# An S4 convolution block with its backward pass: one PSUM pool, fewer table operations, state sums split between VectorE and TensorE

## The chip, the cores and the metric

The kernel runs on one core of one Trainium2 chip. A core has five engines that work side by side and wait for each other through semaphores: TensorE (PE: matmuls, with its weight loads shown as PEld), VectorE (DVE), ScalarE (ACT), GpSimd (POOL) and SyncE (SP). Each takes its own instructions strictly in order. Sixteen DMA engines move data between HBM and the on-chip memory SBUF; here SP's queue issues most transfers and POOL's queue most stores of results. Matmul results land in PSUM, eight banks of 2 KB a partition (512 fp32 numbers), from which only DVE and ACT can read ("eviction"). The metric is the device time of one execution in microseconds (us), the median of the runs.

## The reference

The reference computes a block and all its gradients. `L` = 2048 rows, `D` = 512 channels, `N` = 128 states, `F` = 1792.

```
xn  = layernorm(x)
K[d,l] = Re sum_n C[d,n] * exp(dt[d]*A[d,n]*l) * dt[d]*B[d,n]     # complex A, B, C
s   = irfft(rfft(xn, 4096) * rfft(K, 4096))[:2048] + xn * Dskip   # per channel
g   = silu( silu(xn @ w1) @ w2 )
out = x + s * g
grads of x, A_re, A_im, B_re, B_im, C_re, C_im, log_dt, Dskip, w1, w2 for a given grad_out
```

Inputs and outputs are bf16.

## The kernel before, in words

**Stages.** The channels are taken in four blocks `b` of 128. First come the layer norm (`layer_norm`) and constants (`make_consts`: the transform's sines `TF`, their transposed form `TI`, selection matrices). Then, per block, `gen_tables` makes powers of `exp(dt*A)`: a phase is multiplied out into the scratch area `AR` as int32, shifted so that only the fraction of a turn is left, turned into sine and cosine by one ACT instruction, and multiplied by magnitudes that were stored in HBM. From a few powers (`E`, `Y`, `H`) products give all that the kernel `K` needs; matmuls `ps_k` and `ps_e` sum over the states. `gen_conv_x` transforms a block of `xn` and stores the spectrum in HBM (`Ud`); `gen_conv_fwd` transforms `K`, loads the spectrum (`sp_in`), multiplies (`products`, lines 1046 on) and transforms back. The transforms (`dft_fwd`, `dft_inv`) are two matmul steps each with evictions between (`ps_s`, `ps_i`), and a turn of the middle result by DMA or by PE. Beside all this `gen_ffn_fwd` runs the two forward matrix products (`ps_h`, `ps_o`), 256 rows at a time.

In the middle the gates are formed (`gen_gate_rows`), and the backward convolution (`gen_conv_bwd`, which loads both spectra again) runs beside the backward products `ps_da` and `ps_dx` (`gen_ffn_da`).

Last comes the gradient of the states (`gen_ssm_bwd`): per block `ssm_fold` sums the gradient of `K` into 21 exponents by matmuls with 0/1 matrices and evicts them four times repeated (`Gf`); `ssm_half` multiplies by two masks (`Gb`); then in 16 groups `ssm_v` multiplies by transposed powers (`ps_v`, evicted to `Vb`), `ssm_products` forms four products with `E` (`Tp`, a real and an imaginary pair for every exponent), and `ssm_sums` adds them up over the exponents by 43 matmuls with the identity into `psS`. `gen_ssm_grads` ends each block. Beside it run the weight gradients `gen_dw2` and `gen_dw1` (both `ps_w`; the second reads `dh_tok`, loaded by DMA transposes), and, after the states, the gradient of the layer norm (`gen_ln_bwd`).

**Pools.** PSUM has two pools: `pf`, four tiles of one bank, and `pc`, two tiles of two banks. SBUF pools open and close on a left and a right side; a pool that opens where another one closed waits for it. `gen_ln_bwd` uses a pool on the right, where the states' pool `sb` is. The transforms share four `w8` tiles, used in turn.

**Order.** The body (lines 1743 to 1887) only records operations. `Plan` then simulates the engines with fixed costs and sets the order on every engine, which engine takes an operation recorded as "any" (a copy on DVE or ACT), and which PSUM bank a tile gets. It starts from a random order, improves it by backward and forward passes (`FROM`, `ROUNDS`, `FIRST`, `LAST`), and applies a list of 175 random shifts of priorities, `NUDGES`. The resulting order is fixed in the program. All instructions are issued through one line of `Recorder.emit`, so nearly every row of the profile names L158 (line 158); rows are told apart by the names of their tiles.

Of the kernel before, what the change touches and what calls it, by code (L numbers as in the profile page):

```python
# [12 lines left out]
ACT = mybir.ActivationFunctionType  # L13
# [3 lines left out]
I32 = mybir.dt.int32  # L17
DRAM = bass.MemoryType.DRAM
PSUM = bass.MemoryType.PSUM
P = 128  # L20
PI_LO = 3.1415925
PB = 18
# [70 lines left out]
class Recorder:  # L93
# [13 lines left out]

    def noted(self, engine, op):
        def note(*args, **kw):
            self.ops.append((engine, op, args, kw))  # L110
        return note

    def emit(self, tc, roots, order=None, homes=None, engines=None, heads=None):
# [40 lines left out]
        for n in order or range(len(self.ops)):  # L154
            engine, op, args, kw = self.ops[n]
            if engine == "any":
# [5 lines left out]
        for line in sorted(marks.values(), key=lambda l: l[0][0].space is not None):  # L162
            while line:
                step(line)
# [3 lines left out]
class Plan:  # L168
# [5 lines left out]
    FROM, ROUNDS = (2182906552, 1, 0), 4  # L174
    FIRST, LAST = (22000.0, 3000.0, 1500.0, 80.0, 1200.0), (20660.199999999997, 3000.0, 1500.0, 80.0, 1200.0)
    NUDGES = [(1090443319, 3, 4000), (4118025466, 5, 1000), (1691718919, 5, 2000), (1436320375, 0, 200), (2213169401, 5, 2000),
# [1763 lines left out]
```

## Time and profile before

| | us |
|---|---|
| median of 3 runs | 594.05 |
| lowest, highest run | 593.77, 594.74 |
| span of the profiled execution | 592.6 |
| PE busy in it | 543.2 |
| DVE busy | 519.2 |
| ACT busy | 434.1 |
| POOL busy | 75.8 |

The span runs from the first to the last instruction of the profiled execution. A row of the groups by shape reads: line, engine, operation, output <- inputs, shapes, xcount | busy us of all, mean ns of one | idle us of the engine before them and what ended it. The mean is one instruction's latency; busy divided by the count is smaller, since neighbours overlap. A row of the windows reads: the window, its length, then busy us and (x instructions) of PE, PEld, DVE, ACT and POOL, then the granted PE clock, the DMA engines' busy share, and GB/s. A row of the chain reads: start us, us, engine, tile, line, xcount. A row of waits reads: who waited <- for whom: us in total, times, longest us.

### The profile page before, as it was taken

How to read it: one execution, taken by the hardware profiler on the slowest of the kernel's cores; microseconds unless marked ns; L12 is line 12 of the kernel's file. 1: busy time of each engine (PE TensorE's matmuls, PEld its weight loads, DVE VectorE, ACT ScalarE, POOL GpSimd, SP SyncE). 2: the span in 40 equal slices, each digit the busy share in tenths (PEclk: the TensorE clock that was granted, in tenths of full speed). 3: DMA queues.
4: the chain of work that ended last, by engine and by line, in shares of the span. 5: the costliest groups of instructions: out<-in, count | busy, mean ns of one | idle time of the engine just before them, and what ended most of it. 6: DMA issues, size and time to landing. Idle time of an engine off the chain costs nothing.

```text
span 592.6 us, 14999 instructions
## 1 busy us (share of the span) xinstructions
PE 543.2 (92%) x6208; PEld 400.4 (68%) x6208; DVE 519.2 (88%) x955; ACT 434.1 (73%) x541; POOL 75.8 (13%) x161
## 2 busy tenths in 40 slices
PE   0579999999999995799999999999999999999997
PEld 0456657758567764677667667677887777795586
DVE  9999999999999989999998898468998956387794
ACT  6989899988998989997888858165467454673652
POOL 8131010101001000000001000000002033101221
PEclk9989999999999997799999999999999999999999
DMA  9978999999999989678789965989999999397795
GB/s 225 366 242 247 262 223 361 259 272 319 272 329 268 356 273 318 193 249 189 235 249 308 249 206 163 237 233 167 218 218 270 196 208 272 102 200 204 230 230 145
DMA packets 187029, 144.64 MB, mean 244 GB/s; under 512 B 120080, under 2 KB 167952, under 8 KB 183376
## 3 DMA queue, kind: packets, MB, share of 16 engines
q1 hardware_dynamic: 180528, 125.59, 80.6%
q0 software_dynamic: 6144, 17.83, 9.3%
q8 instruction: 48, 0.79, 0.5%
q10 hardware_dynamic: 288, 0.26, 0.1%
q14 instruction: 21, 0.17, 0.1%
HBM read 55.97 MB, written 58.85 MB: 194 GB/s over the span
## 4 chain that ended last, share of the span: by engine, by line
PE 42%; DVE 11%; issue 2%; DMA 2%; ACT 2%; DVEq 0%; ACTq 0%; SPq 0%
PE ps_w L158 14%; PE ps_da L158 6%; PE ps_dx L158 6%; PE psS L158 5%; PE ps_i L158 4%; PE ps_v L158 3%; DVE sp_in L158 2%; PE pt_t L158 2%; DVE cm L158 2%; DVE g_t L158 1%; DMA sp_in<-Ud 1%; PE ps_s L158 1%; DVE dhT L158 1%; DVE Tp L158 1%; PE G L158 1%
## 5 line engine op out<-in xcount | busy, mean ns | idle before, releaser
L158 PEld LDWEIGHTS <-W 128*128 128x128 bf16 x1008 | 90.5, 99 | 23.9 <-issue 8.3
L158 ACT CAST dA<-ps_s 128x1024 bf16<-128x1024 f32 x85 | 85.3, 1036 | 8.8 <-PE ps_s L158 8.1
L158 PEld LDWEIGHTS <-xn 128*128 128x128 bf16 x512 | 47.9, 99 | 28.3 <-DVE xn L158 21.0
L158 PE MATMUL ps_o<-W,aT 128*128 128x512 bf16 x224 | 59.3, 384 | 3.4 <-ACT XT L158 3.2
L158 PE MATMUL ps_da<-doT,W 128*128 128x256 bf16 x448 | 61.6, 273 | 0.2 <-DVE dhT L158 0.2
L158 PE MATMUL ps_h<-XT,W 128*128 128x256 bf16 x448 | 59.2, 278 | 2.1 <-ACT hT L158 1.5
L158 PE MATMUL ps_dx<-W,dhT 128*128 128x512 bf16 x224 | 58.0, 379 | 0.0
L158 PE MATMUL ps_w<-YD,a_tok 128*128 128x512 bf16 x224 | 56.0, 379 | 0.2 <-ACT a_tok L158 0.2
L158 ACT CAST Vb<-ps_v 128x672 bf16<-128x672 f32 x55 | 38.0, 724 | 23.4 <-PE ps_v L158 14.9
L158 PE MATMUL ps_w<-dh_tok,xn 128*128 128x256 bf16 x448 | 54.1, 273 | 0.1
L158 DVE TENSOR_TENSOR Tp<-Vb,Eb 128x1344 bf16<-128x1344 bf16 x64 | 52.0, 857 | 2.1 <-ACT Vb L158 1.4
L158 PE MATMUL psS<-Tp,ident 128*128 128x128 bf16 (+1 forms) x688 | 47.4, 218 | 0.0
L158 ACT CAST dB<-ps_i 128x1024 bf16<-128x1024 f32 x39 | 38.4, 1017 | 12.1 <-PE ps_i L158 11.7
L158 DVE TENSOR_TENSOR dhT<-ps_da,dhT 128x512 bf16<-128x512 f32 x56 | 38.1, 688 | 8.1 <-PE ps_da L158 8.1
L158 PEld LDWEIGHTS <-ident 128*128 128x128 bf16 x688 | 41.7, 98 | 3.0
L158 PEld LDWEIGHTS <-TF 128*128 128x128 bf16 x384 | 27.6, 103 | 19.1 <-issue 11.3
L158 ACT CAST o<-ps_w 128x256 bf16<-128x256 f32 (+1 forms) x36 | 15.7, 440 | 31.7 <-PE ps_w L158 26.8
L158 PE MATMUL ps_i<-I,sp_in 64*128 64x128 bf16 x768 | 35.9, 220 | 1.4 <-DVE sp_in L158 1.2
L158 PEld LDWEIGHTS <-YD 128*128 128x128 bf16 x576 | 28.9, 98 | 7.9 <-issue 4.4
L158 PEld LDWEIGHTS <-sp_in 64*128 64x128 bf16 x768 | 28.0, 96 | 9.2 <-DVE sp_in L158 4.1
L158 PEld LDWEIGHTS <-aT 128*128 128x128 bf16 x224 | 19.8, 99 | 21.3 <-issue 5.6
L158 PE MATMUL ps_s<-dB,F 128*64 128x512 bf16 x192 | 30.5, 389 | 3.2 <-ACT dA L158 1.9
(225 smaller groups left out, 1197.0 us busy)
## 6 DMA issues: line engine op xcount, KB each, us to landing
Yd<-YD SPq DMA_DIRECT2D x8, 1024.0 KB, 6.4
sp_in<-Ud SPq DMA_DIRECT2D x8, 1024.0 KB, 6.2
Ed<-E SPq DMA_DIRECT2D x8, 672.0 KB, 4.1
Eb<-Ed SPq DMA_DIRECT2D x8, 672.0 KB, 5.6
h_in<-Hd SPq DMA_DIRECT2D x10, 512.0 KB, 4.3
Hd<-hT POOLq DMA_DIRECT2D x8, 512.0 KB, 7.2
Ud<-dA SPq DMA_DIRECT2D x4, 1024.0 KB, 7.1
KXd<-dA SPq DMA_DIRECT2D x4, 1024.0 KB, 6.7
```

The source lines that it names most:

```text
L158: getattr(getattr(nc, engine), op)(*[on(a) for a in args], **{w: on(a) for w, a in kw.items()})
```

## The change

- PSUM becomes one pool `pf` of eight one-bank tiles. Every two-bank tile of the transforms, of `ps_v` and of the fold is replaced by two one-bank tiles, each with its own eviction.
- `gen_conv_fwd` begins with `gen_conv_x` of its block and keeps the spectrum as `k.U`; it is still stored for the backward pass, and no longer loaded in the forward pass.
- Phases are scaled so that a turn is 2^16. The shift is dropped; ACT's sine reads the low 16 bits of each int32 directly. The same is done for the transform's sines. The quarter-turn offset may run on DVE or ACT, and so may the last step of the layer norm.
- `TI` is made by 32 PE transposes with four evictions in place of one DMA transpose.
- In `gen_tables` two pairs of product operations become two double-width ones, and the two halves of `W` one operation.
- `ssm_fold` evicts each exponent sum four times under a 0/1 scale straight into the masked form `Gb`, and its zeroing matmuls go; `ssm_half` makes only the second mask's half.
- `ssm_sums` first combines the real and imaginary products on DVE, in place, and then needs 21 matmuls; a later subtraction goes.
- `gen_ln_bwd`'s pool moves to the left side, beside the states; it writes its result in place, `pd_l` has two buffers instead of four, and `dh_tok` two instead of three.
- The planner gets other starting values, no longer counts an ordering that lies wholly within a tile's own users, and has a list of 28 `NUDGES`.

The core of the diff:

```diff
+    def any_affine(self, out, in_, scale, bias, held):
-    FROM, ROUNDS = (2182906552, 1, 0), 4
-    FIRST, LAST = (22000.0, 3000.0, 1500.0, 80.0, 1200.0), (20660.199999999997, 3000.0, 1500.0, 80.0, 1200.0)
+    FROM, ROUNDS = (3240493571, 0, 60), 5
+    FIRST, LAST = (30000.0, 5000.0, 3000.0, 120.0, 1200.0), (30000.0, 5000.0, 3000.0, 120.0, 1200.0)
...
-            gates = {g for n in u for g in self.shuts[n]}
+            gates = {g for n in u for g in self.shuts[n] if not set(self.order[g][0]) <= set(u)}
...
-        TS(out=ks[:, :, 1, :], in_=prod[:], scalar=8191, op=ALU.bitwise_and)
-        TS(out=prod[:], in_=prod[:], scalar=6144, op=ALU.add)
-        TS(out=ks[:, :, 0, :], in_=prod[:], scalar=8191, op=ALU.bitwise_and)
+        TS(out=prod[:, :, 0], in_=prod[:, :, 1], scalar=-16384, op=ALU.add)
...
-    nc.sync.dma_start_transpose(k.TI[:], k.TF[:].rearrange("p t c k -> p (t c k)"))
+    turned(k, lambda i: k.TF[:].rearrange("p t c k -> p (t c) k")[:, i], 32, k.TI, k.ev)
...
-        for h in range(2):
-            ps = pc.tile([P, 8, P], F32, name="ps_s1", tag="pc")
-            for j in range(8):
+        for h in range(4):
+            ps = k.pf.tile([P, 4, P], F32, name="ps_s1", tag="pf")
+            for j in range(4):
...
-            TS(out=V[:, 0, 0:n], in_=V[:, 1, 0:n], scalar=-float(1 << (PB - 2)), op=ALU.add)
-            TS(out=V[:, :, 0:n], in_=V[:, :, 0:n], scalar=32 - PB, op=ALU.logical_shift_left)
+            nc.any_affine(V[:, 0, 0:n], V[:, 1, 0:n], 1.0, -float(1 << (PB - 2)), k.quarter[:])
...
-            TT(out=m1, in0=lo(x[0]), in1=hi(x[1]), op=ALU.mult)
-            TT(out=m2[:], in0=lo(y[0]), in1=hi(y[1]), op=ALU.mult)
-            TT(out=out(c), in0=m1, in1=m2[:], op=op)
+            TT(out=area.rearrange("p (x m a) -> p x m a", m=8, a=4), in0=lo, in1=hi, op=ALU.mult)
...
+            TT(out=Y[:, c, :, 8:32, :].rearrange("p q j a -> p q (j a)"), in0=pr[0][:, :, c], in1=pr[1][:, :, 1 - c], op=op)
...
 def gen_conv_fwd(k, b):
+    yield from gen_conv_x(k, b)
...
-    U = spectrum_in(k, dft, b, "U")
+    U = k.U
...
-        k.ev(out=Gf[:, :, 16 * bank:16 * bank + n, :],
-                       in_=G21[:, bank, 0:32 * n].rearrange("p (e q) -> p q e", e=n).unsqueeze(3).to_broadcast([P, 32, n, 4]))
+        for h in range(2):
...
+            for a in range(4):
+                nc.any_affine(dst[:, :, :, a], src, k.m4[:, a:a + 1], 0.0, 0.0)
...
 def ssm_sums(k, Tp, out):
-    psS = k.pf.tile([P, 3, 64], F32, name="psS", tag="pf")
+    psS = k.pf.tile([P, 2, 64], F32, name="psS", tag="pf")
+    nc.vector.tensor_tensor(out=Tp[:, 0, :, 0], in0=Tp[:, 0, :, 0], in1=Tp[:, 1, :, 1], op=ALU.subtract)
+    nc.vector.tensor_tensor(out=Tp[:, 0, :, 1], in0=Tp[:, 0, :, 1], in1=Tp[:, 1, :, 0], op=ALU.add)
     for e in range(NE):
-        nc.tensor.matmul(out=psS[:, 0:2], lhsT=k.ident[:], rhs=flat(Tp[:, 0, e]), start=(e == 0), stop=False)
-    for r in range(2):
-        nc.tensor.matmul(out=psS[:, 1 + r:2 + r], lhsT=k.ident[:], rhs=flat(Tp[:, 1, 0, r:r + 1]), start=False, stop=False)
-    for e in range(1, NE):
-        nc.tensor.matmul(out=psS[:, 1:3], lhsT=k.ident[:], rhs=flat(Tp[:, 1, e]), start=False, stop=(e == NE - 1))
+        nc.tensor.matmul(out=psS[:], lhsT=k.ident[:], rhs=flat(Tp[:, 0, e]), start=(e == 0), stop=(e == NE - 1))
...
-        dh = fw.tile([P, k.T, 2, P], BF16, name="dh_tok", tag="dh_tok", bufs=3)
+        dh = fw.tile([P, k.T, 2, P], BF16, name="dh_tok", tag="dh_tok", bufs=2)
...
-    k.pf = ctx.enter_context(Room(nc, "pf", bufs=4, space=PSUM))
-    k.pc = ctx.enter_context(Room(nc, "pc", bufs=2, space=PSUM))
+    k.pf = ctx.enter_context(Room(nc, "pf", bufs=8, space=PSUM))
...
-        yield from woven([gen_tables(k, 0), gen_conv_x(k, 0)], [2, 1])
+        yield from gen_tables(k, 0)
         for b in range(1, 4):
-            yield from woven([gen_tables(k, b), gen_conv_x(k, b), gen_conv_fwd(k, b - 1)], [3, 1, 1])
+            yield from woven([gen_tables(k, b), gen_conv_fwd(k, b - 1)], [3, 1])
...
-    interleave([gen_ln_bwd(k, pool("lw", side="right")), dw], [1, 1])
+    interleave([gen_ln_bwd(k, pool("lw")), dw], [1, 1])
```

More of the change, by code (lines that the diff above doesn't have):

```diff
@@ L21 @@
 PI_LO = 3.1415925
-PB = 18
+PB = 16
 BR, SR, APART = 1.8, 0.5, 5
@@ L980, in dft_fwd @@
             continue
-        pt = pc.tile([P, 16, P], BF16, name="pt_f", tag="pc")
-        for j in range(16):
-            nc.tensor.transpose(out=pt[:, j], in_=A[:, u, j, :], identity=k.ident[:])
-        k.ev(B[:, u], pt[:])
+        for v in range(2):
+            pt = k.pf.tile([P, 8, P], BF16, name="pt_f", tag="pf")
+            for j in range(8):
+                nc.tensor.transpose(out=pt[:, j], in_=A[:, u, 8 * v + j, :], identity=k.ident[:])
+            k.ev(B[:, u, 8 * v:8 * v + 8], pt[:])
     for _ in range(LAG - 1):
@@ L1004, in dft_inv @@
     for q in range(4):
-        ps = pc.tile([P, 2, 4, 32, 4], F32, name="ps_i2", tag="pc")
+        ps = [k.pf.tile([P, 4, 32, 4], F32, name="ps_i2", tag="pf") for _ in range(2)]
         for g in range(4):
@@ L1396, in ssm_fold @@
         nc.sync.dma_start(GE[a:P:4].rearrange("p i t q -> p i (t q)"), k.dKd[b, a].rearrange("i j r -> j i r"))
-    G21 = pc.tile([P, 2, 512], F32, name="G21", tag="pc")
+    G21 = [k.pf.tile([P, 512], F32, name="G21", tag="pf") for _ in range(2)]
     ID, SH, WR, MX = 0, 1, 2, 3
```

150 lines of the change are left out of this document (79 added, 71 removed), and 40 rows, old and new, of the table NUDGES.

## The prediction

> **What bounds the kernel now.** I read the three stages first (windows), then what TensorE (PE) waits for, then the chain that ended last, then the groups of instructions by shape.
>
> ```profile
> core 0: us, PE busy (x) PEld busy (x) DVE busy (x) ACT busy (x) POOL busy (x), PEclk, DMA share, GB/s
> 0.00:240.00 240.00, 202.18 (x2379) 146.05 (x2380) 232.21 (x404) 213.70 (x272) 37.96 (x93) 0.97 0.95 286
> 240.00:390.00 150.00, 143.49 (x1769) 101.16 (x1767) 127.39 (x182) 108.23 (x112) 6.45 (x12) 0.99 0.82 231
> 390.00:593.00 203.00, 197.56 (x2065) 153.24 (x2063) 159.58 (x370) 112.21 (x159) 31.34 (x56) 1.00 0.92 204
> ...
> 205.00:262.00 57.00, 44.44 (x669) 35.12 (x666) 52.00 (x76) 51.58 (x55) 1.12 (x2) 0.88 0.75 247
> ```
>
> There are three regimes. To 240 us (tables, forward convolution, forward feed-forward) VectorE (DVE) is busy 232.2 of 240 us, 97%, and ScalarE (ACT) 89%: both are full, and PE loses 38 us. From 240 to 390 PE is at 96%. From 390 to the end PE is at 97% while DVE has 43 us and ACT 91 us to spare. The hole at 205 to 262, where the last forward convolution hands over to the backward pass, has PE idle for 12.6 us with DVE and ACT at 91%.
>
> ```profile
> PE pt_t L158 <- DVE xn L158: 20.7, 2, 20.1
> ...
> 532.72 2.36 PE psS L158 x43
> ...
> 557.86 24.26 PE ps_w L158 x205
> 582.19 7.16 PE ps_w L158 x64
> ```
>
> PE's only long named wait is the first one, 20.1 us for the layer norm. The chain's end is pure matmul: the state sum of one group is 43 matmuls in 2.36 us, 54.9 ns each, and 31 us of weight gradient close the run. So in the last stage work taken from PE is time, and in the first stage only work taken from DVE and ACT together is.
>
> **Complex sums ahead of TensorE.** Of the 43 identity matmuls of a group 21 stay: 22 x 16 groups x 54.9 ns = 19.3 us of PE go. The fold loses its zeroing matmuls, 4 x (512 + 160) columns at the same 0.43 ns a column, 1.15 us, and gains four small ones: 1.0 us. Together -20.3 us. In exchange DVE gets two in-place operations of 1344 elements per group.
>
> ```profile
> L158 DVE TENSOR_TENSOR Tp<-Vb,Eb 128x1344 bf16<-128x1344 bf16 x64 | 52.0, 857 | 2.1 <-ACT Vb L158 1.4 <-issue 0.5
> L158 DVE TENSOR_TENSOR Gb<-Gf,MK 128x2688 bf16<-128x2688 bf16 x8 | 12.4, 1556 | 0.0
> L158 DVE TENSOR_TENSOR Sa<-Sa 128x256 f32<-128x256 f32 x4 | 1.7, 425 | 8.7 <-ACT Sa L158 8.7
> L158 DVE TENSOR_TENSOR AR<-tau,ecst 128x1024 int32<-128x1024 f32 x8 | 9.8, 1219 | 0.0
> ```
>
> The nearest row is Tp, the same size and type: 52.0 / 64 = 0.81 us, so 32 x 0.81 = 26.0 us. The upper bound is the rate of the slow AR row (1.19 ns an element): 1.60 us, 51 us in all. I take 26.0. DVE gives back half of Gb (8 x (1.55 - 0.81) = 5.9) and the Sa subtraction (1.7). DVE in the last stage: 159.6 + 26.0 - 7.6 = 178.0 us, while PE's end would shrink that stage to 203 - 20.3 = 182.7. That is 97%, beside a PE that is as full, and hardly an order keeps both so busy. But copies that may go to either engine sit there too.
>
> ```profile
> L158 DVE CAST Vb<-ps_v 128x672 bf16<-128x672 f32 x9 | 7.6, 856 | 4.5 <-PE ps_v L158 4.5
> L158 DVE CAST o<-ps_w 128x512 bf16<-128x512 f32 x3 | 2.1, 689 | 11.1 <-PE ps_w L158 11.1
> L158 DVE CAST Gf<-G 128x640 bf16<-128x640 f32 x2 | 1.6, 815 | 0.0
> ```
>
> These 11.3 us on ACT bring DVE to 166.7, 91%. The sums also put 1.6 us of DVE between a group's products and its psS matmuls: a new wait on PE. PE takes its matmuls in order, so behind a late psS stand the next ps_v, for whose eviction ACT and then DVE's next products wait, and ps_w. With two streams (weight gradients and states) to order around that I charge 4 us; bounds 0 and 13 (the 178 us at the 91% that DVE keeps in the hole is 195.6, against 182.7).
>
> **Sines of low halves, fewer table operations.** The shift of the phases goes altogether, the twiddle masks shrink from three operations to one per half, and the pairs of products and of W are merged.
>
> ```profile
> L158 DVE TENSOR_SCALAR AR<-AR 128x2048 int32<-128x2048 int32 x8 | 9.8, 1226 | 0.0
> L158 DVE TENSOR_SCALAR AR<-AR 128x1920 int32<-128x1920 int32 x8 | 9.3, 1160 | 0.0
> L158 DVE TENSOR_SCALAR ks<-prod 128x1024 int32<-128x1024 int32 x4 | 2.7, 684 | 0.0
> L158 DVE TENSOR_SCALAR prod<-prod 128x1024 int32<-128x1024 int32 x2 | 1.4, 690 | 0.0
> L158 DVE TENSOR_TENSOR AR<-YD,H 128x1536 bf16<-128x1536 bf16 x16 | 15.2, 958 | 0.0
> L158 DVE TENSOR_TENSOR m<-YD,H 128x1536 bf16<-128x1536 bf16 x16 | 15.2, 959 | 0.0
> L158 DVE TENSOR_TENSOR W<-E,CT 128x1344 bf16<-128x1344 bf16 x32 | 27.0, 861 | 0.0
> L158 DVE TENSOR_SCALAR xn<-x_sb,rstd,nb 128x512 bf16<-128x512 bf16 x16 | 5.7, 399 | 0.0
> ```
>
> Shift: 9.8 + 9.3 = 19.1 us off DVE. Twiddles: 2.7. Products: Tp to Gb gives 0.52 ns an element, so 3072 cost 1.71 us busy; 16 of them, 27.4, replace 30.4: 3.0. W: 16 at Gb's 1.55 us, 24.8: 2.2. Sum 27.0 us off DVE before 240. The layer norm's rows (xn) and the phase offset may now go to ACT; a 512-wide row costs 0.36 us here against 0.77 for the scaled ACT row below, and I leave them on DVE, at no change; moved, they would take up to 12.3 us of ACT for 5.7 of DVE. The sines read as many elements as before, from a 16-bit half at every second place; no row shows that, and I take no change.
>
> **PSUM as one pool of eight banks.** Every two-bank tile becomes two one-bank tiles with an eviction each.
>
> ```profile
> L158 ACT CAST dA<-ps_s 128x1024 bf16<-128x1024 f32 x85 | 85.3, 1036 | 8.8 <-PE ps_s L158 8.1 <-ACT dK L158 0.4
> L158 ACT CAST hT<-ps_h 128x512 bf16<-128x512 f32 x48 | 27.0, 608 | 3.7 <-PE ps_h L158 2.0 <-DMA Hd<-hT 1.7
> L158 ACT CAST Vb<-ps_v 128x672 bf16<-128x672 f32 x55 | 38.0, 724 | 23.4 <-PE ps_v L158 14.9 <-DVE Tp L158 4.0 <-issue 2.4
> L158 ACT CAST Xr<-ps_k 128x336 bf16<-128x336 f32 x22 | 10.1, 460 | 1.9 <-PE ps_k L158 1.9
> L158 ACT CAST Gf<-G 128x2048 bf16<-128x2048 f32 x4 | 7.5, 1866 | 7.2 <-PE G L158 7.1
> L158 ACT ACTIVATE AR<-AR,m,rstd 128x512 bf16<-128x512 bf16 x16 | 12.3, 812 | 2.5 <-DVE m L158 2.5
> ```
>
> One 1024-column eviction is 85.3 / 85 = 1.00 us; two of 512 are 2 x 0.56 = 1.12. In the first stage 92 tiles are split (64 of the forward transforms, 24 of the inverse, 4 transposes): 11.0 us more on DVE and ACT. [...] In the last stage 64 splits of Vb cost at most 2 x 0.46 - 0.69 = 0.23 us each, 15 us, and 64 masked evictions of 256 or 80 elements replace Gf (9.1 us in the rows shown): each below the 0.77 us of the 512-wide scaled row, so 49 us at most, 29 by the Xr row's 0.46. With 91 us to spare on ACT I take both as hidden; without that slack they would cost 35 us. The middle stage's 76 splits, 9.1 us, hide in the 22.6 us of DVE and 41.8 of ACT that are idle there. What eight interchangeable banks save is not in the trace: at most the 6.5 and 5.4 us that PE idles in the middle and last stages, at least nothing. I take nothing.
>
> First stage in sum: DVE and ACT together 445.9 - 27.0 + 11.0 + 4 (four 1024-wide evictions for the TI table) = 433.9. At the present joint share the 240 us become 233.5: -6.5. Bounds: -22 (DVE alone binds: 232.2 - 27.0 + 5.5 = 210.7, at 97% 217 us) and +11 (ACT alone binds and takes the 15: 228.7 at 91%).
>
> **Input spectrum on chip.** Four reloads go, and the transform of the input moves into the convolution that uses it.
>
> ```profile
> sp_in<-Ud SPq DMA_DIRECT2D x8, 1024.0 KB, 6.2
> TI<-TF SPq DMA_TRANSPOSE x1, 12.0
> ...
> 197.89 0.32 SPq L158 DMA_DIRECT2D Ud<-dA  x1
> 213.53 2.35 DVE L158 TENSOR_TENSOR cm<-sp_in,dA 128x2048 bf16<-128x2048 bf16 x2
> ```
>
> The loads, four of 6.2 us, and the TI transpose of 12.0 leave SP's queue; none of them is a wait of PE in the view of waits, so nothing is gained, and TI's 32 transposes on PE (1.8 us at psS's pace) fall into its first idle 20 us. What is late next is the spectrum: it now holds one of four `w8` slots until the inverse transform has read the product made in it. Block 3's spectrum was stored at 197.9 us, ahead of block 2's products at 213.5; now its first tile must wait for those to be consumed, and behind its matmuls on PE stand those of the feed-forward. Its 16 evictions move into the hole at 205 to 262, where DVE and ACT are at 91%: 16 x 0.56 / 2 = 4.5 us there, won back earlier. I charge 2; bounds 0 and 10.
>
> **Norm gradient beside the state sums.** Its pool moves to the left so that its DVE work need not wait for the states' end; without that the 91% above could not be spread. The price is `dh_tok` at two buffers instead of three.
>
> ```profile
> 557.45 8.42 SPq L158 DMA_TRANSPOSE dh_tok<-DHd  x2
> 568.17 8.78 SPq L158 DMA_TRANSPOSE dh_tok<-DHd  x2
> ...
> dh_tok<-DHd SPq DMA_TRANSPOSE x14, 6.9
> ```
>
> A step of the gradient takes 64 matmuls, 7.16 us. Its two transposes take 8.42 us to issue and 6.9 to land, 15.3 us; behind them on SP's queue stand the last loads and stores. With two buffers a bare step stalls up to 15.3 - 7.16 = 8.1 us. Seven steps spread among 150 us of other PE work hide this; only the last can be bare. I charge 2; bounds 0 and 8.
>
> **Sum.** -20.3 + 4 - 6.5 + 2 + 2 = -18.8; the middle stage I leave as it is. The profiled span 592.6 becomes 573.8; the median of the runs stands 1.45 above that span, so 575.
>
> **Rivals.** *The first stage follows DVE alone.* For it: 97% against ACT's 89%, and 0.95 of the DMA engines' time, eased by four loads. Against: the copies are already dealt between both engines. -22 in place of -6.5 gives 560; with free banks worth 4 more, 556. *DVE takes over the tail.* If the copies stay on DVE: 178.0 us at 91% is 195.6, +13 in place of +4, and without the first stage's gain 591; half of that gain leaves 587. *The transposes bind (slower).* If the state work is finished early and the weight gradient is left alone at the end, each bare step costs 8.1 us; 18.8 + 2 lost is the point where it decides, three bare steps. Three give 575 - 2 + 24.3 = 597, four 605. For it: 31 us of pure weight gradient end the run now, and DMA is at 0.92. Against: those steps now run with no stall. *No change.* The order comes from a new search of the planner. PE's 38 us lost before 240 and 12.6 in the hole are what an order decides; one that loses 19 more gives 594.
>
> **How the numbers follow.** Forecast 0.52 (575, its own range 566 to 583), DVE-only first stage 0.19 (556), DVE tail 0.15 (587), transposes 0.10 (about 600), no change 0.04. The shown runs differ by 0.16%, so 0.2% is about what can be told from none. Faster 0.86, same 0.04, slower 0.10. The range 557 to 590 leaves out about half of the 556 case, the slower one and no change.
>
> **What would show it.** psS at 336 matmuls; two new Tp rows near 0.81 us; in the last stage DVE above 88% and PE still above 95%. No int32 shift rows, ps_s at 512 columns near 0.56 us. DVE before 240 clearly under 97%. Waits of PE on `dh_tok` or of the ps_s transform on a released `sp_in` slot would be the costs I charged; a new DVE row at 1.6 us, or PE under 90% in the last stage, would make the forecast wrong.

## The result and the profile after

The changed kernel takes **619.36 us** (618.16 to 619.45, four runs) against 594.15 us (593.77 to 594.74) for the kernel before on the same chip: 1.0415 of its time, 95% interval 1.040 to 1.043. It is 4% slower. The forecast was 575 us, range 557 to 590: wrong in size and in sign. In the changed kernel nearly all rows name L169, in the kernels of the experiments L160 or L172; it is the same line of `Recorder.emit`. Profiled spans are 1.5 to 1.9 us shorter than the times.

I cut the span at two places that both kernels have: the first `ps_da` (the backward products begin) and the first `G` (the fold of the state gradient begins). In the kernel before, the cut at 260.0 lies 0.2 us ahead of its first `ps_da`. Windows by these stages, of the kernel before:

```profile
0.00:260.00 260.00, 217.97 (x2632) 158.92 (x2633) 251.67 (x432) 232.13 (x289) 38.52 (x94) 0.97 0.92 278
260.00:388.50 128.50, 126.20 (x1502) 87.04 (x1500) 107.94 (x154) 89.70 (x95) 5.90 (x11) 1.00 0.85 238
388.50:592.60 204.10, 199.06 (x2080) 154.49 (x2078) 159.58 (x370) 112.30 (x159) 31.34 (x56) 1.00 0.92 205
```

And of the changed kernel:

```profile
0.00:265.60 265.60, 233.40 (x2700) 177.70 (x2700) 240.87 (x407) 237.33 (x370) 36.83 (x93) 0.96 0.87 260
265.60:403.30 137.70, 137.62 (x1485) 99.73 (x1483) 113.59 (x172) 91.88 (x145) 6.49 (x12) 1.00 0.75 209
403.30:617.60 214.30, 186.43 (x1701) 138.96 (x1701) 175.72 (x407) 126.98 (x268) 31.42 (x56) 0.94 0.88 193
```

Every stage is longer: by 5.6, 9.2 and 10.2 us. In the first two PE is busy 26.9 us more, though the change added no matmul there but the 32 transposes of `TI`, and the order moved about 20 others ahead of the first `G`. In the last it is busy 12.6 us less and the stage is longer all the same. These rows of the groups say that most instructions came at the prices of the prediction:

```profile
L169 ACT CAST dA<-ps_s 128x512 bf16<-128x512 f32 x162 | 86.7, 640 | 3.5 <-PE ps_s L169 3.4
L169 DVE TENSOR_TENSOR AR<-YD,H 128x3072 bf16<-128x3072 bf16 x16 | 27.7, 1752 | 0.0
L169 DVE TENSOR_TENSOR W<-E,CT 128x2688 bf16<-128x2688 bf16 x16 | 24.8, 1552 | 0.8 <-DMA Kd<-KE 0.8
L169 DVE TENSOR_TENSOR Tp<-Tp 128x1344 bf16<-128x1344 bf16 x32 | 26.6, 848 | 0.0
L169 PE MATMUL psS<-Tp,ident 128*128 128x128 bf16 x336 | 25.3, 223 | 6.5 <-DVE Tp L169 6.5
L169 ACT ACTIVATE Gb<-G,m 128x80 bf16<-128x80 f32 (+1 forms) x57 | 27.1, 688 | 7.5 <-DVE Gb L169 6.4 <-PE G L169 1.0
```

The 32 sums cost 26.6 us (26.0 forecast), an eviction of 512 columns 86.7 / 162 = 0.535 us (0.56), the double-width products 27.7 us (27.4), `W` 24.8 (24.8), and `psS` has its 336 matmuls. One group the prediction took as hidden: the masked evictions `Gb`, 27.1 us on ACT alone. What changed for TensorE shows only in single matmuls. The first step of the inverse transform (`ps_i<-I`, 1024 matmuls of 64 rows in all), a stretch of it in the timeline, before:

```profile
128.79 0.22 PE L158 MATMUL ps_i<-I,cm 64*128 64x128 bf16 x2
128.85 0.22 PE L158 MATMUL ps_i<-I,sp_in 64*128 64x128 bf16 x2
128.91 0.22 PE L158 MATMUL ps_i<-I,cm 64*128 64x128 bf16 x2
```

and after:

```profile
128.36 0.23 PE L169 MATMUL ps_i<-I,cm 64*128 64x128 bf16 x1
128.42 0.22 PE L169 MATMUL ps_i<-I,dA 64*128 64x128 bf16 x1
128.48 0.22 PE L169 MATMUL ps_i<-I,cm 64*128 64x128 bf16 x1
```

A new row comes every 56 ns in both, but before it holds two matmuls (x2) and after one (x1). Each of these matmuls uses half of the array's 128 rows: `h` = 0 the upper 64, `h` = 1 the lower. Before, `dft_inv` recorded them alternately into one two-bank tile, and the planner, whose `cells` takes a PSUM tile as one cell, kept that order. After, the halves are two tiles, nothing ties them together, and the planner issues all matmuls of one half and then all of the other: the operands `cm` and `dA` take turns matmul by matmul, where before each came twice in a row, once for each half. Its own cost model makes that free: line 383 charges a matmul of half the rows half the time, whoever its neighbour is.

Waits of PE in the changed kernel:

```profile
PE pt_t L169 <- DVE xn L169: 22.9, 1, 22.9
PE ps_v L169 <- DVE Gb L169: 10.7, 4, 3.8
PE psS L169 <- DVE Tp L169: 6.5, 2, 4.1
```

The second and third are new; both lie in the last stage. What follows in that view is below 3 us.

### The profile page after: what moved, and what is told of

It is laid out like the page before. It is cut to its first block, busy times and chain, and to the rows that moved or that the text cites. A ratio compares the mean times of both kernels' runs of the same rounds, so it can differ in the third digit from the quotient of the medians.

```text
span 617.6 us, 14608 instructions
## 1 busy us (share of the span) xinstructions
PE 557.5 (90%) x5884; PEld 416.4 (67%) x5884; DVE 530.2 (86%) x983; ACT 456.2 (74%) x781; POOL 74.7 (12%) x161
## 5 line engine op out<-in xcount | busy, mean ns | idle before, releaser
L169 PEld LDWEIGHTS <-W 128*128 128x128 bf16 x1008 | 90.3, 98 | 21.9 <-issue 6.4
L169 ACT CAST dA<-ps_s 128x512 bf16<-128x512 f32 x162 | 86.7, 640 | 3.5 <-PE ps_s L169 3.4
L169 PEld LDWEIGHTS <-xn 128*128 128x128 bf16 x512 | 47.3, 99 | 31.1 <-DVE xn L169 22.9
L169 PE MATMUL ps_h<-XT,W 128*128 128x256 bf16 x448 | 60.7, 275 | 1.3 <-DVE XT L169 1.3
L169 PE MATMUL ps_da<-doT,W 128*128 128x256 bf16 x448 | 61.6, 274 | 0.0
L169 ACT CAST dB<-ps_i 128x512 bf16<-128x512 f32 x76 | 42.7, 592 | 23.4 <-PE ps_i L169 22.4
L169 PE MATMUL ps_w<-YD,a_tok 128*128 128x512 bf16 x224 | 58.3, 384 | 0.3 <-ACT a_tok L169 0.3
L169 PE MATMUL ps_dx<-W,dhT 128*128 128x512 bf16 x224 | 58.5, 391 | 0.0
L169 PE MATMUL ps_w<-dh_tok,xn 128*128 128x256 bf16 x448 | 57.7, 273 | 0.7 <-DVE Vb L169 0.7
L169 ACT CAST Vb<-ps_v 128x336 bf16<-128x336 f32 x114 | 42.5, 463 | 19.1 <-PE ps_v L169 11.4
L169 PE MATMUL ps_o<-W,aT 128*128 128x512 bf16 x224 | 55.7, 379 | 0.0
L169 DVE TENSOR_TENSOR Tp<-Vb,Eb 128x1344 bf16<-128x1344 bf16 x64 | 52.1, 850 | 2.0 <-ACT Vb L169 1.7
L169 DVE TENSOR_TENSOR dhT<-ps_da,dhT 128x512 bf16<-128x512 f32 x56 | 37.8, 687 | 11.2 <-PE ps_da L169 10.8
L169 PE MATMUL ps_v<-Gb,YT 128*128 128x168 bf16 x256 | 34.1, 257 | 11.4 <-DVE Gb L169 10.7
L169 PEld LDWEIGHTS <-YT 128*128 128x128 bf16 x256 | 24.6, 107 | 21.4 <-issue 12.3
L169 PEld LDWEIGHTS <-dA 64*128 64x128 bf16 (+1 forms) x384 | 33.0, 104 | 6.3 <-DVE dA L169 3.6
L169 PE MATMUL ps_i<-I,cm 64*128 64x128 bf16 x256 | 33.9, 240 | 2.5 <-DVE cm L169 2.5
L169 ACT CAST o<-ps_w 128x256 bf16<-128x256 f32 (+1 forms) x38 | 17.2, 456 | 25.3 <-PE ps_w L169 20.4
L169 PE MATMUL ps_i<-I,dA 64*128 64x128 bf16 x256 | 32.7, 240 | 2.9 <-DVE dA L169 2.9
L169 POOL DMA_DIRECT2D out_dram<-o x20 | 12.3, 614 | 182.5 <-ACT o L169 166.3
L169 PEld LDWEIGHTS <-dhT 128*128 128x128 bf16 x224 | 21.4, 100 | 18.7 <-issue 1.0
L169 PEld LDWEIGHTS <-aT 128*128 128x128 bf16 x224 | 20.6, 98 | 18.9 <-issue 1.2
```

What stands on the lines that cost most here:

```text
L169: getattr(getattr(nc, engine), op)(*[on(a) for a in args], **{w: on(a) for w, a in kw.items()})
```

## The experiments

Three causes are to be told apart: **1**, the half-row matmuls no longer run in pairs; **2**, the masked evictions of the fold; **3**, the state sums on VectorE and the order of the last stage.

A new plan moves everything, so most runs keep the order of a known plan: the unchanged body is planned as always, every instruction's place in that sequence becomes its key, and the edited body is put in the order of these keys as far as data and banks allow (`frozen`; banks are given anew, first freed, first given). A run in a "planned" order goes through the planner's search instead. Every ratio is to the kernel before, run again on the same chip; its medians lie between 594.2 and 595.7 us.

**Halves alternating again, alone** (`a_pair`), and **the kernel before without the alternation** (`b_unpair`):

```diff
+    for c in plan.halves():
+        for a, b in zip(c[::2], c[1::2]):
+            back[b] = (back[a][0] + 0.5, back[b][1])
+        chains.append(c)
```

```diff
+    for c in plan.halves():
+        at = sorted(back[n][0] for n in c)
+        chains.append(c[::2] + c[1::2])
+        for n, x in zip(chains[-1], at):
+            back[n] = (x, back[n][1])
```

> The changed kernel with one thing put back: the 1024 half-row matmuls of the first inverse step are issued alternately again, one of the upper 64 rows, then one of the lower, as in the kernel before; every other instruction keeps its place in the order as nearly as the banks allow, and nothing is computed differently. Theory 1 (lost pairing): in the trace of the changed kernel these matmuls go one per 56 ns, before they went two per 56 ns, which is 1024 x 28 ns = 28.7 us of TensorE; between half and all of it lies on the path, so 590 to 604 us. Theory 2 (masked evictions of the fold) and theory 3 (VectorE's two sums per group and the order of the tail): TensorE's first inverse step is not what binds, 617 to 621 us.

> The kernel before with one thing taken away: in each pair of halves all matmuls of the upper rows are issued, then all of the lower; everything else stays in its place. Theory 1: up to 28.7 us more TensorE time, between half and all of it on the path: 609 to 623 us, and the groups of ps_i with I add up to about 95 to 100 us of busy time instead of 53. Theories 2 and 3: at most 2 us, 594 to 596 us.

Measured: **600.41 us**, 1.0112 of the kernel before (1.0093 to 1.0130), so 19.0 us off the changed kernel; and **613.42 us**, 1.0315 (1.0272 to 1.0357), 19.2 us on top of the kernel before. The two are mirror images. The timeline of `a_pair` shows the pairs again:

```profile
125.53 0.22 PE L172 MATMUL ps_i<-I,cm 64*128 64x128 bf16 x2
125.59 0.22 PE L172 MATMUL ps_i<-I,dA 64*128 64x128 bf16 x2
```

and the page's sums of busy time, with the same matmuls, of the changed kernel

```profile
PE 557.5 (90%) x5884; PEld 416.4 (67%) x5884; DVE 530.2 (86%) x983; ACT 456.2 (74%) x781; POOL 74.7 (12%) x161
```

and of `a_pair`:

```profile
PE 531.2 (89%) x5884; PEld 391.8 (65%) x5884; DVE 527.8 (88%) x983; ACT 452.9 (76%) x781; POOL 74.6 (12%) x161
```

26.3 us of PE go, near the 28.7 expected, and 19.0 of them are time. Most of it comes ahead of the first `G`: that falls from 403.3 to 387.1 us, while the stage behind it only goes from 214.3 to 211.8. The expectation for `b_unpair` that the groups add up to 95 to 100 us was off: they show 75.8, and PE as a whole goes from 543.2 to 557.4, 14.2 us. (That trace is of its fastest run, 608.77 us, which is 14.6 us above the kernel before.) Groups that alternate overlap one another, so their sums were a poor measure; the whole engine's is the better one. Cause 1 is shown, from both sides: two matmuls in 56 ns where the halves alternate, one where they do not. Why it takes the turns no run here tests. In the kernel before, PE's 6208 matmul rows start, by their tiles, in the program's order; in the changed kernel 38 of 5884 do not, all half-row matmuls where the issue goes from one half to the other. There the rows hold two for a while (x2 from 122.08 to 122.48).

**The old fold in the changed kernel, alone** (`a_fold`):

```diff
-            for a in range(4):
-                nc.any_affine(dst[:, :, :, a], src, k.m4[:, a:a + 1], 0.0, 0.0)
+        k.ev(out=Gf[:, :, 16 * bank:16 * bank + n, :], in_=ov.rearrange("p e q -> p q e").unsqueeze(3).to_broadcast([P, 32, n, 4]))
...
+    k.nc.vector.tensor_tensor(
+        out=Gb[:].rearrange("p w q x -> p q w x"), in0=Gf[:, 16 * h:16 * h + 16].rearrange("p q e a -> p q (e a)").unsqueeze(2).to_broadcast([P, 16, 2, NE * 4]),
+        in1=k.MK[:].rearrange("p w e a -> p w (e a)").unsqueeze(1).to_broadcast([P, 16, 2, NE * 4]), op=ALU.mult)
```

> The changed kernel with the fold of the kernel before: two broadcast evictions of all four copies and one masked multiply of 2688 elements for each half, in place of 16 masked evictions and a multiply of 1344; the halves stay apart, the sums stay on VectorE, the order is kept. Theory 2: the 16 evictions of a fold run one after another for 8 us ahead of the first ps_v (11.2 us from the first G to it, 7.7 before) and take 27 us of ScalarE; putting the old fold back wins 4 to 10 us: 609 to 615 us. Theories 1 and 3: within 2 us of the changed kernel, 617 to 621 us, since VectorE gets 8 x 0.7 us more for the wider multiply.

Measured: **608.68 us**, 1.0247 (1.0225 to 1.0269): 10.7 us off the changed kernel, 0.3 us beyond the fast end of its range. The stage behind the first `G` falls from 214.3 to 203.8 us; ahead of it nothing moves. How the masked evictions held things up is in the timeline of the changed kernel, first fold, ACT

```profile
404.56 0.86 ACT L169 ACTIVATE Gb<-G,m 128x256 bf16<-128x256 f32 x1 [0.81 <-PE G L169]
406.31 0.86 ACT L169 ACTIVATE Gb<-G,m 128x256 bf16<-128x256 f32 x1 [0.89 <-DVE Gb L169]
408.06 2.89 ACT L169 ACTIVATE Gb<-G,m 128x256 bf16<-128x256 f32 x5 [0.89 <-DVE Gb L169]
```

and DVE:

```profile
405.45 0.82 DVE L169 TENSOR_SCALAR Gb<-G,m 128x256 bf16<-128x256 f32 x1 [1.72 <-ACT Gb L169]
407.20 0.82 DVE L169 TENSOR_SCALAR Gb<-G,m 128x256 bf16<-128x256 f32 x1 [0.93 <-ACT Gb L169]
```

The two engines wait for each other in turn instead of working side by side: 404.56, 405.45, 406.31, 407.20, 408.06, each start 30 to 40 ns behind the other engine's end. The four masks read one `G` tile and write every fourth element of the same stretch; which of the two ties the engines together is taken up under `a_major`. PE's `ps_v` stands behind the last of them.

**Both put back** (`a_pair_fold`), the two edits above together:

> The changed kernel with both things put back, the alternating half-row matmuls and the fold of the kernel before; the rest of its order is kept. Apart they took 619.4 to 600.4 us (19.0) and to 608.7 us (10.7). If they are two separate causes in two stages (up to the first G of the fold, and behind it), they add: 588 to 592 us. If one hides behind the other: 596 to 600 us. If what is left is still above 594 us, a third part of the change costs time.

Measured: **590.39 us**, 0.9908 (0.9869 to 0.9948). 19.0 and 10.7 make 29.7; together they give 29.0. The causes add, and with both out of the way the rest of the change is 0.9% faster than the kernel before, 4 us, not the 19 of the forecast. This is in the changed kernel's own order. Windows of its three stages:

```profile
0.00:256.60 256.60, 216.96 (x2682) 161.17 (x2702) 239.99 (x408) 235.44 (x370) 36.64 (x93) 0.99 0.91 269
256.60:386.30 129.70, 125.53 (x1485) 88.64 (x1483) 112.68 (x171) 89.99 (x145) 6.46 (x12) 1.00 0.81 223
386.30:590.20 203.90, 182.05 (x1685) 137.43 (x1701) 178.49 (x401) 110.50 (x218) 31.31 (x56) 0.97 0.94 203
```

The last stage is the open one: PE is busy 17.0 us less than before (182.05 against 199.06; 16 matmul records are missing from this trace, and `a_fold`, which misses none, has 182.89). The prediction took 20.3 from it, and the stage is as long as before, 203.9 against 204.1. The work taken from PE turned into idle time.

**Why one masked eviction is slow** (`a_major`): four separate blocks instead of every fourth element, order of the changed kernel kept, halves apart.

```diff
-    Gb = [sb.tile([P, 2, 16, NE * 4], BF16, name="Gb", tag="Gb", bufs=3) for _ in range(2)]
+    Gb = [sb.tile([P, 2, 4, 16, NE], BF16, name="Gb", tag="Gb", bufs=3) for _ in range(2)]
...
-                                 rhs=Gb[:, :, q0 + q + u], start=True, stop=True)
+                                 rhs=Gb[:, :, :, q0 + q + u].rearrange("p w a e -> p w e a"), start=True, stop=True)
```

> The changed kernel with another layout of the masked fold: the four masks write four separate blocks (mask, row, exponent) instead of every fourth element, and TensorE reads them back through a stride; the order is kept, the halves stay apart. If the waits between the 16 evictions come from their interleaved outputs (each waits for the other engine's, 12.7 us on VectorE and 6.4 us on ScalarE), they go, and the first ps_v comes 7 to 9 us after the first G instead of 11.2. If the price of an eviction (885 ns for 256 elements, against 463 ns for 336 of ps_v) comes from the stride of what it writes, it falls to 400 to 450 ns; if from the stride of the PSUM side, it stays at 850 to 900 ns. Time: 611 to 616 us if the waits alone go, 607 to 612 us if the price falls too, 618 to 624 us if TensorE reads the stride at a loss.

Measured: **658.34 us**, 1.1059, far above all three ranges. The eviction's price falls, though not to the 400 to 450 ns expected, but the kernel takes 39 us more. Groups of `a_major`:

```profile
L172 PE MATMUL ps_v<-Gb,YT 128*128 128x168 bf16 x256 | 84.9, 461 | 4.2 <-DVE Gb L172 3.9 <-ACT Vb L172 0.2
L172 ACT ACTIVATE Gb<-G,m 128x256 bf16<-128x256 f32 x27 | 11.2, 494 | 3.5 <-DVE Gb L172 2.7 <-PE G L172 0.7
```

The same two groups in the changed kernel:

```profile
L169 PE MATMUL ps_v<-Gb,YT 128*128 128x168 bf16 x256 | 34.1, 257 | 11.4 <-DVE Gb L169 10.7
L169 ACT ACTIVATE Gb<-G,m 128x256 bf16<-128x256 f32 x27 | 19.3, 885 | 5.1 <-DVE Gb L169 4.1 <-PE G L169 1.0
```

An eviction of 256 elements takes 494 ns where it wrote its blocks and 885 where it wrote every fourth element (DVE 487 and 822), with the same strided PSUM side: the price is on the output side. These are latencies; busy time for each on ACT is 0.41 us (11.2 / 27) against 0.71 (19.3 / 27). The first `ps_v` comes 8.6 us after the first `G` instead of 11.2. The turns did not go with the interleaved outputs: in the timeline of `a_major` the same first five evictions start at 403.60 (ACT), 404.11 (DVE), 404.63 (ACT), 405.14 (DVE) and 405.66 (ACT), each again behind the other engine's end. So the turns do not come from the interleaving; that the masks share one PSUM tile and one output tile is left to suspect, and no run parts these two. But TensorE, which now reads its moving operand in steps of 336 elements, needs 84.9 us for the 256 matmuls instead of 34.1. Why steps cost that much, on either side, was not shown.

**The state sums in kept orders**: put into the kernel before (`b_sums`, the diff of `ssm_sums` shown ahead of the prediction), and taken out of `a_pair_fold` (`a_pf_nosums`, the same diff backwards).

> The kernel before with the two in-place sums alone: VectorE adds the complex parts right behind its products, TensorE sums 21 matmuls for a group instead of 43, the last difference goes; the rest of the order is kept. The recorded prediction (19.3 us of TensorE saved, 4 us lost to VectorE) expects 577 to 583 us. Theory 3 (VectorE has no room): from 390 to 592 us VectorE is busy 159.6 of 202 us already; 32 sums at 0.81 us make it 185.6, more than the 182 us that would be left, so the wait for the sums takes the place of the saved matmuls: 592 to 615 us, with TensorE's longest waits on Tp from VectorE.

> The changed kernel with the alternating halves and the old fold in the kept order (590.4 us), and the state sums on TensorE alone, put where its 21 matmuls were. The converse of the run that gave the kernel before VectorE's sums in its own order (+27.8 us). If VectorE's sums by themselves cost time, taking them away wins: 570 to 586 us. If the kept order is made for them, so that taking them away costs as putting them in did: 598 to 612 us.

Measured: **622.02 us**, 1.0475 (1.0436 to 1.0513), 27.8 us worse; and **600.40 us**, 1.0079, 10.0 us worse than the same order with the sums. The first is above both of its ranges, the second within the range of "the kept order is made for them". Two windows of `b_sums`:

```profile
450.00:480.00 30.00, 19.55 (x177) 14.08 (x177) 27.58 (x54) 14.36 (x19) 4.87 (x9) 0.85 0.96 215
510.00:540.00 30.00, 29.99 (x286) 23.37 (x285) 15.61 (x47) 16.34 (x23) 6.10 (x11) 1.00 0.37 115
```

and its waits of PE:

```profile
PE psS L160 <- DVE Tp L160: 27.8, 12, 6.6
```

In a fixed order PE reaches `psS` before the sums are made and stands, with the next `ps_v` behind it: from 450 to 480 it is busy 19.55 of 30 us, where in the kernel before it is busy all 30. (The low 15.61 us of DVE at 510 to 540 is no sign of this; the kernel before has 13.65 at 480 to 510.) Going the other way costs too. So a kept order does not answer for work moved from one engine to another: here it punished it in both directions. The question has to be put to planned orders.

**Planned orders.** For the changed kernels the planner was told of the pairs, and of the measured price of the masked evictions where they are in; in the kernel before a two-bank tile ties the halves already:

```diff
+        for c in self.halves():
+            i = self.uses[c[1]][0]
...
+            self.uses[c[0]].append(i)
+            self.tiles[i][1].insert(0, c[0])
+            for a, b in zip(c, c[1:]):
...
+                    self.pred[b].append(a)
```

`FROM` and `NUDGES` were searched anew for each; the lists came out at 9 to 32 shifts, and that the searches came equally far is assumed. `b_plan` is the kernel before, `b_sums_plan` the same with the sums on VectorE; `a_pair_plan` is the whole change; the three `a_pf` kernels have the old fold and 16, 8 or none of their 16 groups summed on VectorE.

> A control: the kernel before, no instruction changed, its order searched anew with the same effort as the other two planned ones. It tells what a new order is worth by itself: TensorE is busy 543.2 of 592.6 us, so little can be won, 588 to 598 us on every theory.

> The kernel before with the two sums for a group on VectorE, and the order planned for them. The same sums in the kept order gave 622.0 us, with 27.8 us of TensorE's waits for Tp. If VectorE simply has no room (185.6 us of work in what would be a tail of 182 us), a new order does not help much: 600 to 620 us. If the order was at fault: below 590 us, with TensorE's 19.3 us saved in part. Between these: as much lost as won, 590 to 600 us.

> The changed kernel whose order is planned anew, by a planner that is told two things: the half-row matmuls are issued alternately, both banks of a pair taken at once, and a masked eviction costs 600 ns (256 elements) or 210 ns (80), as measured back to back in the trace of the changed kernel. All instructions of the change stay. Theory 3b (the order is made for wrong costs, and the rest of the change is worth what the prediction said: 6.5 us in the first stage, 16 us in the tail): 570 to 582 us. If VectorE has no room for the 32 sums in any order: 590 to 600 us, as with the alternation alone.

> The changed kernel with the alternating halves and the old fold, its order planned anew with pairs kept; all 16 groups of the state sums have their complex parts added on VectorE. The kept order gave 590.4 us, with TensorE idle for 22 and VectorE for 25 of the 204 us behind the first G. If that idle time is a matter of the order: 575 to 586 us. If the exchange between the engines sets it: 586 to 592 us. The control (a new order of the kernel before took 606 us instead of 594) says that a new order can also be worse by 12 us: then 595 to 605 us.

> The same, but every second group is summed by TensorE alone, as in the kernel before (43 matmuls): VectorE does 16 sums less (13.3 us), TensorE 176 matmuls more (9.7 us). If VectorE's sums are what costs, this is 3 to 10 us faster than with all 16 groups on VectorE; if they win what the prediction said (19.3 us for 4), 5 to 9 us slower; if neither engine binds, within 3 us.

> The same with all 16 groups summed by TensorE alone: VectorE does 32 sums less (26.6 us), TensorE 352 matmuls more (19.3 us). If VectorE's sums are what costs: 5 to 20 us faster than with all groups on VectorE; if they win what the prediction said: 10 to 19 us slower; if neither engine binds, within 4 us.

The three right columns are of the profiled run alone, which for `a_pfs0_plan` is the slowest of five (594.23 us) and for `a_pair_plan` the fastest of four (584.15):

| planned kernel | us | of before (95%) | first `ps_da` | to first `G` | behind it |
|---|---|---|---|---|---|
| `b_plan` | 606.41 | 1.0174 (1.0127 to 1.0221) | 267.6 | 127.5 | 209.6 |
| `b_sums_plan` | 611.61 | 1.0256 (1.0205 to 1.0307) | 269.9 | 129.5 | 210.9 |
| `a_pair_plan` | 587.93 | 0.9866 (0.9797 to 0.9935) | 258.5 | 124.2 | 199.7 |
| `a_pf_plan`, 16 on DVE | **579.96** | 0.9739 (0.9711 to 0.9766) | 253.7 | 125.5 | 200.3 |
| `a_pfs8_plan`, 8 | 583.07 | 0.9792 (0.9756 to 0.9829) | 255.1 | 124.0 | 199.9 |
| `a_pfs0_plan`, none | 590.30 | 0.9904 (0.9885 to 0.9923) | 260.6 | 130.8 | 201.0 |

The control missed its range: a new order alone made the kernel before 1.7% slower, so orders differ by some 10 us for reasons that have nothing to do with the edit, and a planned kernel is to be held against the control rather than against 594. The control starts from the same random order as the kernel before and has 30 shifts where that one has 175; the changed kernel has 28. So part of what the change was charged with may be a less refined order, a rival that no run here settles: held against the control, `a_pf_plan` is 26 us faster and `a_pfs0_plan` 16, and all three `a_pf` kernels are some 9 us shorter in the last stage, if that assumption holds.

`a_pf_plan` is the version that beats both kernels: 2.6% faster than the one before, within the 575 to 586 that its theory asked, and 5 us off the forecast of 575. That nearness is in part luck: its stages win 6.3, 3.0 and 3.8 us, and the forecast had nothing in the middle and 14.3 in the last. `a_pair_plan` missed its 570 to 582 and the rival's 590 to 600. `b_sums_plan` is in the range of "no room", but only 5.2 us above its control. By their medians the three `a_pf` kernels say that the sums on VectorE win 10 us, as the ranges for "they win what the prediction said" have it for `a_pfs0_plan`; `a_pfs8_plan`, at 3.1 us, lies between two of its ranges.

The stages say something else: behind the first `G`, where the sums are, the three are within 1.1 us; what sets 590 apart lies ahead of it, where the three kernels hold the same instructions. Windows of the last stage, with all sums on VectorE

```profile
379.20:579.50 200.30, 184.75 (x1714) 136.62 (x1714) 176.88 (x404) 112.25 (x218) 31.31 (x56) 0.98 0.95 216
```

and with none:

```profile
391.40:592.40 201.00, 194.84 (x2053) 152.15 (x2053) 165.55 (x393) 104.55 (x198) 31.33 (x56) 1.00 0.90 207
```

10 us less on PE, 11 more on DVE (of the sums' 26.6; ACT does 8 us more here), the same length. In the stage where they lie the sums neither win nor lose, in these two orders. Whether the time won ahead of it is an effect of the sums or the luck of the search these runs cannot tell.

**What sets the last stage then.** Three runs in the order of `a_pf_plan`, each with one resource freed: the two sums left out (`r_dve`), 19 of the 21 summing matmuls left out (`r_pe`), the transposing loads of `dh_tok` made plain (`r_dma`).

```diff
+    if not nc.relief:
+        nc.vector.tensor_tensor(out=Tp[:, 0, :, 0], in0=Tp[:, 0, :, 0], in1=Tp[:, 1, :, 1], op=ALU.subtract)
+        nc.vector.tensor_tensor(out=Tp[:, 0, :, 1], in0=Tp[:, 0, :, 1], in1=Tp[:, 1, :, 0], op=ALU.add)
```

```diff
+        if nc.relief and 0 < e < NE - 1:
+            continue
         nc.tensor.matmul(out=psS[:], lhsT=k.ident[:], rhs=flat(Tp[:, 0, e]), start=(e == 0), stop=(e == NE - 1))
```

```diff
-            nc.sync.dma_start_transpose(dh[:, :, j, :], k.DHd[2 * f + j])
+            nc.sync.dma_start(dh[:, :, j, :], k.DHd[2 * f + j].rearrange("p (t q) -> p t q", q=P))
```

> The fastest version so far (alternating halves, old fold, order planned anew; 579.96 us) with its order kept, and the 32 sums of the complex parts on VectorE left out (the state gradients then lack the products' imaginary parts). It frees 26.6 us of VectorE behind the first G. If VectorE sets the length of that stage: 8 to 26 us faster, 554 to 572 us. If TensorE or the DMA engines set it: 577 to 580 us.

> The same version and order, and 19 of the 21 summing matmuls of each group left out (the sums over the exponents then hold two terms only): 304 x 54.9 ns = 16.7 us less for TensorE behind the first G, about what the change itself took from it. If TensorE sets the length: 8 to 17 us faster, 563 to 572 us. If VectorE or the DMA engines set it: 577 to 580 us.

> The same version and order, and the 14 transposing loads of dh_tok replaced by plain loads of the same bytes (the second weight gradient is then taken of the wrong layout). If the DMA engines, busy 0.95 of the time behind the first G, or SP's queue, in which a pair of transposes takes 8.4 us to issue, set the length: 4 to 15 us faster, 565 to 576 us. If TensorE or VectorE set it: 577 to 581 us.

Measured: **577.83**, **580.30** and **579.56 us** (0.9710, 0.9763 and 0.9750 of the kernel before, intervals of 0.003 to 0.005 to each side), against 0.9739 with nothing freed. All three lie within 0.3 us of the ranges for "another sets it". Windows from the first `G` of `a_pf_plan` to 577.0, of `r_dve`

```profile
379.20:577.00 197.80, 182.74 (x1705) 136.26 (x1702) 154.41 (x372) 111.64 (x217) 31.33 (x56) 0.98 1.00 218
```

and of `r_pe` (its span ends at 581.6, but no engine is busy in it behind 577.0):

```profile
379.20:577.00 197.80, 175.58 (x1412) 121.87 (x1410) 177.16 (x405) 111.95 (x218) 31.32 (x56) 0.95 0.98 218
```

DVE is 22 us emptier, or PE 9 (of the 16.7 expected, at a granted clock of 0.95 against 0.98), and the time stays within about 2 us. In this order no single one of the reliefs shortens the stage. That of the DMA engines was small: their share goes from 0.95 to 0.91, and the bytes are the same. With PE at 92% of that stage, DVE at 88% and the DMA engines at 95%, the chain that ended last shows where the time goes when one is freed. In `r_dve`, from 378 to 535, TensorE holds over 70% of it, with `ps_w`, `ps_dx`, `psS` and `ps_v`, and the DMA engines 7%. In `r_pe` it lies almost wholly on VectorE from 500 to 537:

```profile
500.78 9.22 DVE Tp L172 x12
514.54 9.22 DVE Tp L172 x12
537.66 6.99 PE ps_w L172 x33
```

What comes behind that, the rest of the weight gradient, takes the same 42.3 us in `a_pf_plan`, `r_dve` and `r_dma`. So the traces point to TensorE and VectorE together, each nearly full up to there; a run that frees both was not made, and what exactly holds the 200 us is not settled.

## Why the prediction was wrong

Against the span the prediction had -18.8 us, the result is +25.0: 44 us apart.

- **"Every two-bank tile becomes two one-bank tiles with an eviction each", and "the middle stage I leave as it is".** This is the step that failed worst: 19 us. The evictions cost less than it says (two of 0.535 us for one of 1.00 on ACT: 0.07 us a split, not 0.12). But a two-bank tile also tied the two halves of a transform to one order, and this was priced nowhere. The row was there to see, `x2` in the timeline, for the one group of matmuls that uses half the array.
- **"64 masked evictions ... each below the 0.77 us of the 512-wide scaled row ... I take both as hidden."** Wrong by 10.7 us. The bound held: with 27.1 us on ACT and about 5 on DVE they lie within the 29 and 49 us named. In busy time the 256-wide ones cost 0.71 us each, above the 0.46 of the Xr row and below 0.77. What failed is "hidden": "91 us to spare on ACT" is an answer about an average, while the 16 evictions of a fold stand in one chain ahead of the first `ps_v`, ACT and DVE in turn, and PE waits 10.7 us behind them.
- **"In the last stage work taken from PE is time", and the charge of 4 us for the sums.** -20.3 + 4 became 0: 16 us. The prices were near (PE some 16 to 17 us less with halves and fold put back, the sums 26.6 us). I had worked out that DVE would reach 178.0 of 182.7 us, called it an order hardly to be found, and then talked it down by moving copies to ACT; with halves and fold put back it is 178.5. The stage kept its 204 us, 200 in the best order. The sign that I had named, PE under 90% in the last stage, came: 87% in the changed kernel. The rival "DVE takes over the tail" had the place right; but emptying DVE wins next to nothing either, so it too named one engine where two or three are nearly full. How much of these 16 us is the less refined order stays open.
- **First stage, -6.5.** In the changed kernel +5.6, of which 8.2 are the halves. With them paired it is -2.6 (257.4 against 260.0), and -5.1 from the first matmul on, which came 2.5 us later (22.6 against 20.1). The way was right and less than half of the size came. VectorE before 240 is busy 222.8 us, 93%, as its sign had asked, but over that stage DVE and ACT together lose 8.3 us with the halves paired, where the sum has 12.0, and the later start of PE was not in it. Two of its bounds are off by their own figures: 217 us is -23, not -22, and ACT at its own 89% would give 257 us, not 251.
- **Spectrum and `dh_tok`, +2 each.** In the changed kernel's view of waits no wait of PE is named on a spectrum's slot and none on `dh_tok`; the third rival, bare transposes, did not come, though it alone put a time above 594, and plain loads win nothing. What the two parts cost by themselves was not measured.
- **The rival "no change", by a looser order,** was the nearest in kind, at 0.04. The control shows how much an order alone can do: some 10 us.

Put together by the profiled spans: halves and fold are 27.4 us (617.6 against 590.2 with both put back). The other 16.4 are the stages with both put back: the last -0.2 in place of -14.3 (-20.3 + 4 + 2), which is 14.1; the first -3.4 in place of -4.5 (-6.5 + 2), 1.1; the middle +1.2 in place of nothing.

## What to carry to other kernels

When a tile is split, ask what the one tile held in order, beside what its evictions cost: here the halves of TensorE ran in pairs where they were issued in turn (two matmuls in 56 ns) and mostly singly where they were not (one in 56 ns), and this planner kept the turns only where a tile tied them or it was told. Price an operation by a row that writes and reads memory in the same steps, not by one of the same width (the same 256 elements took ACT 885 ns or 494 here), and ask whether it stands in a chain that something waits for: there the spare average hid nothing of PE's 10.7 us. Where two or three resources are each near 90% of a stage, work taken from one can become idle time, as it did here (17.0 us less of PE in a last stage of 203.9 us against 204.1), so sum what the stage can lose with all of them at once. Try a shift of work between engines in a planned order beside a planned control: in kept orders it cost 27.8 and 10.0 us here, and new orders alone differ by some 10.

## What the hardware showed beside that

Two matmuls of 64 rows on different halves of the array, issued in turn, take 56 ns together (`before`, `a_pair`), two on the same half 112 (`after`, one every 56). An eviction of 256 elements that writes bf16 at every fourth element takes 885 ns on ACT and 822 on DVE (`after`), one that writes blocks 494 and 487 (`a_major`): 390 and 335 ns more, in latency, and 0.30 us more of busy time on ACT. In `a_major` that eviction reads PSUM in steps of 32 numbers in its 494 ns, and ACT's copy of 256 contiguous ones from `ps_w` takes 375; the two differ in more than the steps, so the 119 ns between them are no price of the steps alone. A moving operand read in steps of 672 bytes takes 332 ns a matmul of 168 columns (84.9 / 256, `a_major`) instead of 133 (34.1 / 256, `after`).

The granted clock was lower in some windows in which TensorE stood in the midst of a run: in the two windows of `b_sums` it is 0.85 where PE is busy 19.6 of 30 us and 1.00 where it is busy throughout, in the last stage 0.94 after (PE busy 186.4 of 214.3 us) against 1.00 before (199.1 of 204.1). A window's idle time alone does not tell it: in the first 30 us of the kernel before PE is busy 8.9 us at a clock of 1.00, and from 240 to 270 of the changed kernel 28.3 us at 0.70. The matmuls of `psS` take 240 ns in the mean in `b_sums` and 223, up to 314, in the changed kernel, against 219 and at most 220 in the kernel before. So a stall may have been paid twice, once as idle time and once in the matmuls around it; that the stalls lowered the clock, and how much of the 25 us is the second part, these runs do not show.
